# A fused attention and gated feed-forward kernel: one match-row copy moved to ScalarE's queue, one copy moved to VectorE, and the written-out order laid out anew

## The chip, the core and the metric

The kernel runs on one core of one Trainium2 chip. A core has a matrix engine (TensorE, PE in the profile), a vector engine (VectorE, DVE), a scalar engine for activations (ScalarE, ACT), a general engine (GpSimd, POOL) and a synchronization engine (SyncE, SP). SP, ACT and POOL each have a queue from which they start DMA transfers; all transfers are carried by the same 16 DMA engines. Every engine works through its own instructions in their order and waits for the others through semaphores. Times are microseconds of device time of one execution; lower is better.

## What the kernel computes

Attention with routing comes first. Queries and keys are each assigned to the nearest of 16 centroids of their head, and a query sees only the keys of its own centroid. The result feeds a feed-forward layer with a sigmoid gate. Shapes: q, k, v are 4 x 8 x 768 x 64 (batch, head, position, dimension); the tokens are 3072 x 512, the weights 512 x 1536, 512 x 1536 and 1536 x 512.

```python
q_assign = argmax(einsum('bhsd,hcd->bhsc', q_n, c_n), -1)      # q_n, k_n, c_n: normalized
k_assign = argmax(einsum('bhsd,hcd->bhsc', k_n, c_n), -1)
mask = q_assign[:, :, :, None] == k_assign[:, :, None, :]
scores = where(mask, q @ k.T / sqrt(D), -1e9)
attn = softmax(scores) @ v
x = attn.transpose(0, 2, 1, 3).reshape(3072, 512)
out = (sigmoid(x @ w_gate) * (x @ w_val)) @ w_out
```

## The kernel before

**Tiles.** Two heads make a pair, and a batch has four pairs. A pair's queries and keys stand transposed in two tiles, `even` and `odd` (the positions stand in six chunks of 128, and the tiles hold the even and the odd chunks; the columns are the two heads' halves of 384): rows 0 to 63 hold the values, rows 64 to 79 hold the one-hot match rows of the assignment, scaled so that one product of 80 rows gives a score that already carries the mask. The exponentials (L957, ACT) turn score banks `sc` into `es` tiles, the value products (L985, PE) sum them with the V tiles `vp` into the bank `av`; V carries a column of ones, so the sum of the exponentials comes with it. DVE divides (L1010, L1015) into `xn`, which is turned to `x`, mostly by a transposing DMA on SP's queue (L1043), for a few blocks by PE (L1023). The feed-forward part takes x in groups of 256, 512 and then 384 tokens: gate and value projections (L1081) into three banks `ring`, tanh on ACT (L1097), the product on DVE (L1108) into `hT`, the out projection (L1136), a copy on ACT (L1153), a store on SP.

**Match rows.** For the first pair, `prepare_first` (L819) turns keys and queries on PE (L837), copies the four halves out of the banks (L846, a table in line 842 says on which engine: all on ACT), multiplies with the block of centroids (L884), and DVE turns these scores, takes maxima, compares and writes the match rows (`place`, L688, by L515). `place` writes the odd queries' rows first into spare rows of `even` and then copies them to `odd` by a 24 KB DMA (L706, on SP). The other three pairs of batch 0 go through `prepare_pair` (L713: L729, L736 or L518, L769). The later batches go through `prepare` (L520): for two pairs together, matches by L625, and match rows brought by eight DMAs, `even` or `odd` from `oht`; the first two pairs of batch 1 are turned on PE (L555), the others are loaded as quarters (96 KB DMAs in runs of 32 numbers) and turned on DVE (L536). There the rows of `odd` are brought from `even` by a DMA of 192 KB (L592). The DMAs started through the helper `dma` carry its line, 292, in the profile.

**Centroids.** c1 to c5 (L360 to L377) normalize the centroids; c5 turns them on PE (L373), and DVE places them (L382).

**The order.** The kernel does not write its instructions in the order of its loops. Each piece of work is a task with an engine, a length, what it needs, what buffers it takes and a due time (class `Order`, L38). `schedule` (L109) simulates the engines: on each engine, of the tasks that could start first (within 0.02 us), the one with the earliest due time goes next; the queue on SP lets only two of the quarter loads (pkt 13) be under way. `transfers` (L74) shares the DMA time among the queues, with fixed costs in `DMA_START` and `DMA_LAND`. After nine rounds the emitted order is fixed for every engine. Due times come from `due_at` (L277: a line of the place in the attention, with another slope before slot 96) and `due_ffn` (L280), with offsets where work is added.

**What the change touches.** `Order.schedule`, `due_at`, `due_ffn`, the issue lengths (`ISSUE`, L288, and `dma`, L290), `load_nat` (L396), `prepare`'s quarter copies (L541), the match-row due time (L681), `place` (L706), `prepare_first`'s table (L842), `attend` and its end (L919 to L1065), `feed` (L1068), the weight due times `WT` (L1177), `prepare_pair`'s due times (L1188) and the loads of the next batch (L1195 to L1216).

## Time and profile before

| what | value |
|---|---|
| median of 3 runs (lowest, highest) | 325.28 us (324.61, 325.47) |
| the profiled execution's own time | 325.91 us |
| its span | 324.1 us |
| PE busy | 315.6 us, 97% |
| ACT busy | 224.6 us, 69% |
| DVE busy | 147.0 us, 45% |
| POOL busy | 76.2 us, 24% |
| DMA moved | 36.94 MB, mean 114 GB/s |
| mean granted TensorE clock | 0.995 |

The profile is one execution. Its span runs from the first to the last instruction that is recorded; the execution's own time is 1.8 us longer. The busy shares are means over stages that differ: the first 40 us hold the loads and the setup of batch 0, the middle interleaves attention with the feed-forward part, and from about 270 us on the feed-forward part runs alone. In a row of the timeline, the first number is the start, the second how long the merged instructions took, and the bracket tells how long the engine had stood before and what ended that. Rows with SPq or POOLq are DMA issues on these queues.

### The profile page before, as it was taken

The page shows a single profiled execution, that of the slowest core. Times are in us where ns is not written, and L with a number is a line of the kernel's source. Part 1 is how long each engine was busy: PE and PEld are TensorE (multiplying, and loading weights), DVE is VectorE, ACT ScalarE, POOL GpSimd, SP SyncE. Part 2 cuts the span into 40 slices and gives each one's busy share as a digit, 9 for nine tenths or more (in the row PEclk, how much of TensorE's full clock was granted, in tenths as well). Part 3 has the DMA queues.
Part 4 walks back from the last instruction along what each step waited for, and adds up shares of the span by engine and source line. Part 5 has one row for each costly group of instructions (what it writes and reads, how often), then busy time and mean ns, then how long its engine had stood idle before and what let it go on. Part 6 is the DMA issues. An engine that isn't in the chain of part 4 may idle for free.

```text
span 324.1 us, 7275 instructions
## 1 busy us (share of the span) xinstructions
PE 315.6 (97%) x2869; PEld 193.0 (60%) x2869; DVE 147.0 (45%) x344; ACT 224.6 (69%) x326; POOL 76.2 (24%) x121
## 2 busy tenths in 40 slices
PE   8879999999999999999999999999999999999996
PEld 3547888645545656566565655666556665654653
DVE  3859743564954068732433965233113331430430
ACT  5669999438749879797787775888878873332422
POOL 4879661862133115000304061000000000000000
PEclk9979999999999999999999999999999999999999
DMA  6999999947567884226687845200120001002002
GB/s 219 350 248 232 231 218 209 150 98 164 94 145 143 154 156 133 56 48 107 141 185 146 153 104 115 69 15 14 47 77 14 13 14 65 34 0 95 5 0 97
DMA packets 80273, 36.94 MB, mean 114 GB/s; under 512 B 65072, under 2 KB 75056, under 8 KB 80240
## 3 DMA queue, kind: packets, MB, share of 16 engines
q1 hardware_dynamic: 72944, 25.05, 33.1%
q0 software_dynamic: 6864, 11.01, 17.2%
q8 instruction: 22, 0.36, 0.5%
q10 hardware_dynamic: 432, 0.43, 0.4%
q14 instruction: 11, 0.09, 0.1%
HBM read 28.34 MB, written 6.29 MB: 107 GB/s over the span
## 4 chain that ended last, share of the span: by engine, by line
PE 90%; ACT 4%; DMA 3%; DVE 1%; issue 1%; SPq 0%; ACTq 0%
PE ring L1081 38%; PE ring L1136 19%; PE sc L938 18%; PE av L985 10%; ACT es L957 4%; PE sc L625 3%; DMA odd<-even 2%; DMA nat<-in_k_dram 1%; DVE even L515 0%; PE ring L769 0%; PE ring L555 0%; PE ring L884 0%; PE ring L837 0%; DVE ohf L504 0%; PE ring L729 0%
## 5 line engine op out<-in xcount | busy, mean ns | idle before, releaser
L957 ACT ACTIVATE es<-sc,nbias 128x768 f16<-128x768 f32 (+1 forms) x188 | 166.5, 918 | 34.8 <-PE sc L938 33.1
L1108 DVE SCALAR_TENSOR_TENSOR hT<-gt,ring 128x384 f16<-128x384 f32 (+2 forms) x96 | 53.1, 553 | 99.9 <-PE ring L1081 97.4
L1081 PE MATMUL ring<-x,wv 128*128 128x384 f16 (+2 forms) x384 | 78.1, 326 | 0.0
L1081 PE MATMUL ring<-x,wg 128*128 128x384 f16 (+2 forms) x384 | 78.1, 325 | 0.0
L1097 ACT ACTIVATE gt<-ring 128x384 f32<-128x384 f32 (+2 forms) x96 | 47.1, 490 | 32.6 <-DVE hT L1108 16.8
L1136 PE MATMUL ring<-wo,hT 128*128 128x512 f16 (+2 forms) x300 | 69.5, 370 | 0.0
L985 PEld LDWEIGHTS <-es 128*128 128x128 f16 x1152 | 54.9, 97 | 20.7 <-ACT es L957 0.5
L985 PE MATMUL av<-vp,es 128*128 128x65 f16 x1152 | 59.9, 193 | 0.2 <-ACT es L957 0.2
L1081 PEld LDWEIGHTS <-wg 128*128 128x128 f16 x384 | 35.8, 97 | 22.8
L1081 PEld LDWEIGHTS <-wv 128*128 128x128 f16 x384 | 34.8, 97 | 22.0 <-issue 1.2
L1136 PEld LDWEIGHTS <-hT 128*128 128x128 f16 x300 | 27.9, 97 | 27.2
L588 POOL CAST even<-t 128x768 f16<-128x768 f32 x24 | 19.9, 831 | 87.1 <-DVE t L536 69.5
L1153 ACT ACTIVATE osb<-ring 128x512 f32<-128x512 f32 (+2 forms) x25 | 14.5, 580 | 24.7 <-PE ring L1136 24.6
L938 PEld LDWEIGHTS <-even 80*128 80x128 f16 x216 | 19.5, 98 | 15.2 <-issue 6.2
L938 PE MATMUL sc<-odd,even 80*128 80x384 f16 x96 | 26.5, 332 | 1.7 <-DMA odd<-even 1.7
L938 PE MATMUL sc<-even 80*128 80x384 f16 (+2 forms) x120 | 26.5, 294 | 1.1 <-POOL even L757 0.6
L938 PE MATMUL sc<-even,odd 80*128 80x384 f16 (+2 forms) x120 | 26.2, 293 | 0.0
L938 PE MATMUL sc<-odd 80*128 80x384 f16 x96 | 25.9, 327 | 0.2 <-ACT es L957 0.2
L938 PEld LDWEIGHTS <-odd 80*128 80x128 f16 x216 | 19.5, 98 | 9.8 <-issue 1.8
L1010 DVE RECIPROCAL rr<-av 128x6 f32<-128x6 f32 (+2 forms) x36 | 6.8, 190 | 36.9 <-PE av L985 36.7
L536 DVE STREAM_TRANSPOSE t<-nat 128x384 f32<-128x384 f32 x40 | 20.6, 550 | 5.0 <-DMA nat<-in_k_dram 4.8
L462 POOL CAST vp<-nat 128x384 f16<-128x384 f32 x32 | 15.9, 538 | 15.2 <-PE av L985 7.8
(75 smaller groups left out, 168.6 us busy)
## 6 DMA issues: line engine op xcount, KB each, us to landing
out_dram<-osb SPq DMA_DIRECT2D x23, 256.0 KB, 2.1
nat<-in_v_dram POOLq DMA_DIRECT2D x12, 384.0 KB, 4.7
nat<-in_k_dram SPq DMA_DIRECT2D x32, 96.0 KB, 3.0
nat<-in_q_dram SPq DMA_DIRECT2D x32, 96.0 KB, 3.5
odd<-even SPq DMA_DIRECT2D x12, 192.0 KB, 3.8
nat<-in_k_dram SPq DMA_DIRECT2D x5, 384.0 KB, 6.3
nat<-in_q_dram SPq DMA_DIRECT2D x5, 384.0 KB, 7.7
nat<-in_v_dram SPq DMA_DIRECT2D x4, 384.0 KB, 7.6
```

Of the source, the lines that this page charges most:

```text
L462: lambda e=e: nc.gpsimd.tensor_copy(vps[i % NVP][:, e, :, 0:D], buf.tile[:, e, :, :]),
L536: nc.vector.transpose(t[:, half * QB : (half + 1) * QB].rearrange("p (c x) -> p c x", x=128), blocks_[:, half],)
L588: nc.gpsimd.tensor_copy(t[:, NM[nm], cols], t32[p, nm].tile[:, cols])
L625: nc.tensor.matmul(out=ps[32 * g : 32 * g + 32, half, :QB], lhsT=cblk[:, 2 * p + half, :], rhs=t32[p, nm].tile[:, half * QB : (half + 1) * ...
L938: nc.tensor.matmul(out=ps[:, i // per, i % per * N : (i % per + 1) * N], lhsT=kb.tile[0:80, 0, e * QB + j // 2 * 128 : e * QB + (j // 2 + ...
L957: i = nc.scalar.activation(take(es)[:, : together * N].rearrange("p (u c) -> p u c", u=2), sc.tile[:, :, : per * N], AF.Exp, bias=nbias, s ...
L985: nc.tensor.matmul(out=av.tile[:, g : g + D + 1], lhsT=es.tile[:, i * N + c * 128 : i * N + (c + 1) * 128], rhs=vp[:, e, j, :], start=firs ...
L1081: nc.tensor.matmul(out=ps[:, :N], lhsT=ws[fc // FPG][:, dcc, fc % FPG, :], rhs=xb.tile[:, dcc, :N], start=(dcc == 0), stop=(dcc == NDC - 1),)
L1097: lambda rg=rg, gt=gt: nc.scalar.activation(take(gt)[:, :N], rg.tile[:, :N], AF.Tanh, scale=0.5),
L1108: nc.vector.scalar_tensor_tensor(t[:, fc, :N], gt.tile[:, :N], 1.0, rv.tile[:, :N], ALU.add, ALU.mult)
L1136: nc.tensor.matmul(out=ps[:, : m1 - m0], lhsT=hb.tile[:, fc, tb * 128 : (tb + 1) * 128], rhs=wos[fc // FPG][:, fc % FPG, m0:m1], start=(fc ...
L1153: lambda rg=rg, osb=osb, w=m1 - m0: nc.scalar.mul(take(osb)[:, :w], rg.tile[:, :w], 0.5),
```

## The change

It has three parts. The copy of the odd queries' match rows of the first pair is issued on ACT's queue instead of SP's; for the other pairs it stays on SP. The copy of the first pair's second query half out of its bank is made by DVE instead of ACT. The rest changes what the planner assumes and when work is due, and so the order on every engine: engines are free from 0.7 us on, the queue of POOL lets eight transfers be under way, issue lengths and some transfer lengths are other numbers, a set of quarter copies on DVE may not start before the last set has, and due times move. No instruction is added or taken away; the numbers of instructions stay the same on each engine but for the one copy and the one issue.

```diff
+    ROOM = {"SP": 2, "POOL": 8}
...
-        free = {e: 0.0 for e in {t.eng for t in self.tasks}}
-        order, ends = [], []
+        free = {e: 0.7 for e in {t.eng for t in self.tasks}}
+        order, under_way = [], {"SP": [], "POOL": []}
...
-            if t.pkt == 13 and t.eng == "SP":
+            if t.dma and (t.eng == "POOL" or t.eng == "SP" and t.pkt == 13):
+                ends = under_way[t.eng]
                 ends.append(
-                    start + self.DMA_START["SP"] + t.dma if t.landing is None
+                    start + self.DMA_START[t.eng] + t.dma if t.landing is None
                     else start + t.landing - self.DMA_LAND
                 )
-                if len(ends) > 1:
-                    free["SP"] = max(free["SP"], sorted(ends)[-2])
+                room = self.ROOM[t.eng]
+                if len(ends) >= room:
+                    free[t.eng] = max(free[t.eng], sorted(ends)[-room])
...
-    S1, T1 = 96, 51.1
+    S1, T1 = 96, 51.6
-        return T1 + (slot - S1) * (0.442 if slot < S1 else 0.78)
+        return T1 + (slot - S1) * (0.42 if slot < S1 else 0.823)
-        return 36 + work * 1.8
+        return 36 + work * 1.6
-    ISSUE = {"SP": 0.62, "ACT": 0.68, "POOL": 0.85}
+    ISSUE = {"SP": 0.62, "ACT": 0.45, "POOL": 0.76}
...
-                        seq=[cp[p, nm, 0]] if half else [], acq=[] if half else [t32[p, nm]],
+                        seq=[cp[p, nm, 0]] if half else in_turn[-1:],
+                        acq=[] if half else [t32[p, nm]],
                         uses=[natb[b, p, nm]] + ([t32[p, nm]] if half else []),
                     )
+                    if half:
+                        in_turn.append(cp[p, nm, 0])
...
         m = dma(
-            "SP", lambda: od_.tile[64:80, NM["q"], :], lambda: ev.tile[80:96, NM["q"], :], 0.1,
+            "SP" if p else "ACT", lambda: od_.tile[64:80, NM["q"], :],
+            lambda: ev.tile[80:96, NM["q"], :], 0.1,
...
-            on = {("k", 0): "ACT", ("k", 1): "ACT", ("q", 0): "ACT", ("q", 1): "ACT"}[nm, h]
+            on = {("k", 0): "ACT", ("k", 1): "ACT", ("q", 0): "ACT", ("q", 1): "DVE"}[nm, h]
...
-        early = slot < 72.0
+        early = slot < 66.0
-                    due - (28.0 if early else 0.0), lat=0.25,
+                    due - (28.5 if early else 0.0), lat=0.25,
-            due + (-3.1 if last else 4.0) - (18.0 if early else 0.0), lat=0.25 if last else 0.0,
+            due + (-2.6 if last else 4.0) - (23.5 if early else 0.0), lat=0.25 if last else 0.0,
...
-                    "DVE", 0.1 + 0.4 * w, gated, [g2, v1], due - 15.5, lat=0.2, seq=done[:1],
+                    "DVE", 0.1 + 0.4 * w, gated, [g2, v1], due - 11.5, lat=0.2, seq=done[:1],
...
-    WT = (14, 16, 22, 24, 27, 31.5, 38.0, 36, 39)
+    WT = (14, 20.0, 23.5, 24.0, 25.5, 31.0, 38.0, 34.0, 35.0)
...
-        prepare_pair(0, p_, 6.0 * p_, 0.32, (('k', 'q'), (), ('k', 'q'))[p_ - 1], p_ in (1, 2, 3))
+        prepare_pair(0, p_, (0, 6.5, 7.5, 14.0)[p_], 0.31, (('k', 'q'), (), ('k', 'q'))[p_ - 1], p_ in (1, 2, 3))
...
-                            b + 1, p_, nm, "POOL" if (b, grp[0]) == (0, 2) else "SP", max(due - 36.0, 20),
-                            due - 60 if b else 42 if grp[0] else 17.5,
+                            b + 1, p_, nm, "POOL" if (b, grp[0]) == (0, 2) else "SP", max(due - 32.0, 20),
+                            due - 60 if b else 40.0 if grp[0] else 21.5,
-                prepare(b + 1, grp, max(due - 32, 44) + (10 if (b, grp[0]) == (0, 2) else 0), 1.0)
+                prepare(b + 1, grp, max(due - 23.0, 43.5) + (8.0 if (b, grp[0]) == (0, 2) else 0), 1.15)
...
-                    load_v(b + 1, p_, "POOL", due - 26.5, due - 15, due - 39.5)
+                    load_v(b + 1, p_, "POOL", due - 26.5, due - 15, due - 36.0)
```

The due times of the normalization and the turn of x go from 16.0 to 17.5 before the block's, those of batch 0's V casts 6 us later, the match rows' offset from 20 to 22, a POOL quarter's issue from 1.1 to 0.74 and its transfer from 0.55 to 0.7, and a first load's transfer from 0.8 to 0.65.

More of the change, by code (lines that the diff above doesn't have):

```diff
@@ L287 @@
     Q = {"SP": nc.sync, "ACT": nc.scalar, "POOL": nc.gpsimd}
-    ISSUE = {"SP": 0.62, "ACT": 0.68, "POOL": 0.85}
+    ISSUE = {"SP": 0.62, "ACT": 0.45, "POOL": 0.76}
     def dma(eng, out_of, in_of, size, deps=(), due=0.0, acq=(), uses=(), early=0.0, seq=(), pkt=65, lat=0.0):
         return od.add(
-            eng, (1.1 if eng == "POOL" else 0.69) if pkt == 13 else ISSUE[eng], lambda: Q[eng].dma_start(out=out_of(), in_=in_of()),
+            eng, (0.74 if eng == "POOL" else 0.69) if pkt == 13 else ISSUE[eng], lambda: Q[eng].dma_start(out=out_of(), in_=in_of()),
             deps, due, acq=acq, uses=uses, dma=size, early=early, lat=lat, seq=seq, pkt=pkt,
@@ L407, in load_nat @@
                         lambda e=e: src[b, 2 * p + e].rearrange("(p c) d -> p c d", c=NCH),
-                        0.8, (), due[e], acq=[] if e else [buf], uses=[buf] if e else [],
+                        0.65, (), due[e], acq=[] if e else [buf], uses=[buf] if e else [],
                         seq=nat[b, p, nm][:],
@@ L428, in load_nat @@
                         lambda a=a: parts[a // 2, a % 2],
-                        0.55, (), due, acq=[] if a else [buf], uses=[buf] if a else [],
+                        0.7 if eng == "POOL" else 0.55, (), due, acq=[] if a else [buf], uses=[buf] if a else [],
                         early=early, seq=nat[b, p, nm][:1], pkt=13, lat=2.0,
@@ L679, in prepare @@
                                 0.04 if split else 0.07,
-                                [a5, shifted[b, p, half]], due - (20 if (b, grp[0]) == (1, 0) else 0),
+                                [a5, shifted[b, p, half]], due - (22.0 if (b, grp[0]) == (1, 0) else 0),
                                 uses=[oht, aug[b, p][e]], lat=1.5,
@@ L1046, in turn_by_dma @@
             )
-        t4 = od.add("DVE", 0.17 + 0.02 * nq, rec, [t3], due - 16.0, lat=0.05, acq=[rr], uses=[av])
-        t5 = od.add("DVE", 0.14 + 0.15 * nq, norm, [t4], due - 16.0, lat=0.2, acq=[xn], uses=[av, rr])
+        t4 = od.add("DVE", 0.17 + 0.02 * nq, rec, [t3], due - 17.5, lat=0.05, acq=[rr], uses=[av])
+        t5 = od.add("DVE", 0.14 + 0.15 * nq, norm, [t4], due - 17.5, lat=0.2, acq=[xn], uses=[av, rr])
         if not ((b, gr) == (0, 0) and p >= 2 or block == blocks[-1]):
@@ L1058, in attend @@
             return together
-        t6 = od.add("PE", 0.02 + 0.06 * nq, turn, [t5, c_ident16], due - 16.0, lat=0.25, acq=[rg], uses=[xn])
+        t6 = od.add("PE", 0.02 + 0.06 * nq, turn, [t5, c_ident16], due - 17.5, lat=0.25, acq=[rg], uses=[xn])
         xd.append(
             od.add(
-                "DVE", 0.1 + 0.133 * nq, out_of_bank, [t6], due - 16.0, lat=0.2, seq=xd[:1],
+                "DVE", 0.1 + 0.133 * nq, out_of_bank, [t6], due - 17.5, lat=0.2, seq=xd[:1],
                 acq=[] if xd else [xb], uses=[rg] + ([xb] if xd else []),
@@ L1174 @@
         load_nat(0, p_, "q", "SP", -7.9 + p_, behind=nat[0, p_, "k"])
-        load_v(0, p_ - 1, "SP", -7.8 + p_, 9.0 + 4.5 * p_, behind=nat[0, p_, "q"])
-    load_v(0, NP - 1, "SP", -7.7 + p_, 9.0 + 4.5 * NP, behind=nat[0, NP - 2, "v"])
-    WT = (14, 16, 22, 24, 27, 31.5, 38.0, 36, 39)
+        load_v(0, p_ - 1, "SP", -7.8 + p_, 15.0 + 4.5 * p_, behind=nat[0, p_, "q"])
+    load_v(0, NP - 1, "SP", -7.7 + p_, 15.0 + 4.5 * NP, behind=nat[0, NP - 2, "v"])
+    WT = (14, 20.0, 23.5, 24.0, 25.5, 31.0, 38.0, 34.0, 35.0)
     n = 0
```

4 lines of the change are left out of this document (2 added, 2 removed).

## The prediction

> **What bounds the kernel now.** I read the slices of the page first, for where TensorE (PE) and its clock are not full; then the busy times by stage; then the timeline of 4 to 27 us for the one hole they show; then the DMA issues around it, for why.
>
> ```profile
> PE   8879999999999999999999999999999999999996
> ACT  5669999438749879797787775888878873332422
> PEclk9979999999999999999999999999999999999999
> ```
>
> PE is full from the fourth slice to the last; the first three slices, and there the third one's clock, are what is left to win.
>
> ```profile
> 16.00:17.00 1.00, 0.35 (x3) 0.18 (x3) 0.96 (x3) 0.49 (x1) 1.00 (x2) 1.00 1.06 366
> 17.00:18.00 1.00, 0.00 (x0) 0.00 (x0) 0.92 (x3) 0.00 (x0) 1.00 (x3) 0.96 1.15 319
> 18.00:19.00 1.00, 0.98 (x4) 0.47 (x4) 0.19 (x1) 0.15 (x1) 0.94 (x2) 0.50 1.21 208
> 24.00:32.00 8.00, 7.23 (x100) 5.78 (x99) 7.34 (x21) 8.00 (x11) 7.40 (x11) 1.00 0.92 239
> ...
> 80.00:120.00 40.00, 40.00 (x361) 21.79 (x350) 19.32 (x42) 29.00 (x39) 8.88 (x14) 1.00 0.72 137
> ```
>
> Columns: stage, length, busy time of PE, its weight loads, DVE, ACT, POOL, then the clock and the DMA engines. From 16.4 to 18.0 PE and ACT both stand, and at 18 the clock halves; 18 to 21 stays at 0.50, 21 to 22 averages 0.84. From 24 on ACT is full (8.00 of 8), from 42 PE is (40.00 of 40), and it stays so until 321.1, with 3.0 us for the last copy and store. So nothing after 42 us gains unless the work before it gets there sooner, and anything new that stops PE after 42 costs its full length.
>
> ```profile
> 12.07 1.11 ACT L957 ACTIVATE es<-sc,nbias 128x1024 f16<-128x1024 f32 x1 [1.52 <-PE sc L938]
> 13.40 2.12 ACT L957 ACTIVATE es<-sc,nbias 128x1024 f16<-128x1024 f32 x2 [0.21 <-PE sc L938]
> ...
> 18.02 1.12 PE L938 MATMUL sc<-odd,even 80*128 80x384 f16 x3 [1.66 <-DMA odd<-even]
> ...
> 18.85 1.69 ACT L957 ACTIVATE es<-sc,nbias 128x768 f16<-128x768 f32 x2 [1.92 <-PE sc L938]
> ```
>
> The hole is one wait: the scores of the first pair's odd queries wait for their match rows (odd<-even), a DMA.
>
> ```profile
> nat<-in_v_dram SPq DMA_DIRECT2D x1, 384.0 KB, 8.2
> odd<-even SPq DMA_DIRECT2D x1, 24.0 KB, 6.2
> ```
>
> Issued on SP at 11.79, 24 KB land 6.2 us later, at 17.97; the 384 KB load issued before them on the same queue (9.6) lands at 17.8. The rows stood behind loads, not behind their own size.
>
> **The change, part by part.** My sum is made on the profiled execution, 325.91 us (span 324.1, and 1.8 around it); it stands 0.63 above the median, 325.28.
>
> 1. *The start of the first pair.* In the new instruction order the turn of the centroids (L373, waits for DVE until 5.28) goes ahead of the second key turn, which ran at 4.77. The turn is then at 5.34, and the keys and both queries at 5.48, 5.89 and 6.30 (three transposes 0.41). With 0.59 from turn to copy (4.77 to 5.36) ACT's last two copies end at 6.56 and 7.00, and the second query half, now on DVE (0.53 to 0.56 there, 0.49 on ACT), runs 6.89 to 7.44 instead of ending at 6.91. So +0.53 for the match chain on DVE: its first rows are ready at 11.1, not 10.56, the last even query half at 12.3. PE in turn waited until 11.41 for a load, so its next matches (L769) come only 0.1 later and the first exponential starts at 12.26 (+0.19). ACT's table load moves from 6.92 to 7.00.
>
> 2. *The rows' issue on ACT.* In ACT's order it stands behind the first exponential, which ends at 13.37; the rows it reads are ready by 12.3, so it does not wait. Price: ACT's issues in the trace took 0.41 (centroids) and 0.93 for two; bounds 0.41 and SP's 0.61, I take 0.45. Behind it on ACT stand the second and third exponentials, which end at 16.0 instead of 15.52, and for the third the value products wait; these end at 16.25. On SP, the issue goes (0.6), and so does the first early key load of the next batch, which ran at 12.49: its four loads now stand together behind the first transposing DMA, at about 19.3 to 20.8.
>
> 3. *The landing.* A 24 KB row copy behind loads on ACT's queue is not in the trace. Nearest rows: 1.9 us on an emptier queue (66 to 71 us), 3.3 and 4.1 at 25 to 27 us, 6.2 here; ACT's own first load took 2.8. I take 3.0, since ACT's queue holds nothing else: 13.4 + 3.0 = 16.4. Between 1.9 and 6.2 it lands at 15.3 to 19.6; below 16.25 nothing more is won, since PE is busy until then. [...]
>
> 4. *PE and its clock.* The odd scores start at 16.45 instead of 18.02. 3.4 us at half clock cost 1.7 us of PE time; with 0.2 us of idle left instead of 1.66 I expect full clock. [...]
>
> 5. *To the steady stage.* The fourth exponential comes at 17.0 instead of 18.85. Six exponentials (0.85) and four copies (0.49) follow until pair 1's first long one: 17.0 + 7.06 = 24.1, and 0.35 for the third pair's match scores (0.85, L769), which now stand before its scores: 24.45 instead of 25.94, 1.5 us gained. From there ACT ran 14.21 us without a gap; its work is the same, so PE's full stage begins 1.5 us sooner.
>
> 6. *The new order after that.* Same 2,869 products, so its price is only new waits. I measured in PE work, at the chain's paces (65-column product 0.73/24 us, 384-column 0.65/4), how far each consumer stands behind its producer. Score to value products: nowhere under 1.3 us after 36 us of work (1.22 before). Match scores (L625) to the first scores that use them: 10.9, 14.5, 14.5, 14.3, 13.9, 14.3 us (before 12.7, 13.6, 19.3, 18.7, 23.5, 22.4). The needed chain is DVE's eight steps (4.1 to 7), row issues (0.62 each, up to six) and 1.9 to 3 us to land: 10 to 13 us against the odd scores 1 to 1.5 us behind the first. It fits each time, by 1 to 2.5 us. On POOL's queue the second weight (wv) now follows a V load and four casts, so it is issued at about 20.3 instead of 16.3 and lands by 29.8 (9.5 us as before), long before its use at 39.2 (40.7 - 1.5). The first part of wo comes last of the three; the transfer that held that place on POOL's queue before landed at 58.8 (issued 42.2, 16.6 to land), and its use is at 61.2 (62.7 - 1.5). All of this I put at 0, bounds -0.5 and +1.5: cover is the room named, and where it is gone PE stops for what is missing.
>
> The end is unchanged. Sum: 325.91 - 1.5 = 324.4 profiled, and on the median 325.28 - 1.5 = 323.8. In PE work alone the place at 24.3 us would be 2.2 us better, as the third pair's match scores are done by then; ACT's stage gives 0.7 of that back.
>
> **The rivals.**
> - *The first projections wait for the transposed x (slower).* x0's second part goes by transposing DMA on SP; before, it is issued at 31.3 and lands at 38.4, 0.65 ahead of the first projection at 39.05. Now four loads (1.5 MB) stand on SP's queue from 19.3. If they drain by 27.7 (the same bytes as before, with the DMA engines' hole at 28 to 29 filled, 43 and 19 GB/s), x0 lands near 37.0, in time for 37.6 (39.05 - 1.5). If they drain at 31, two transposing DMAs of 4.9 and 4.5 us put it at 40.4: PE stops 2.8 us, net +1.3, 326.6. It decides from a landing of about 39.1 on, where the gain is gone. For it: x DMAs that took 6 to 7 us and halve the rate (205 GB/s at 18 to 23, 390 after). Against: the producer is issued 2 us sooner.
> - *The rows land no sooner on ACT's queue.* 6.2 us from 13.4 is 19.6, fourth exponential at 20.2, 1.3 later than before, clock still dropped: 326.6. For it: DMA engines full (1.06). Against: they landed 0.17 us behind the load before them on SP, as things in one line do. [...]
> - *Hidden or given back.* ACT's full stage or x0 as the gate lets only 0.5 us through: 324.8. For it: PE loses only 1.4 us between 25 and 42, so two engines must both move up.
> - *A new stop in the full stage*, such as the stores (which wait for ACT's copy of the out projection) now ahead of the match rows on SP, once or twice 1 us: 324.8 to 325.8.
>
> **How the numbers follow.** My forecast, a gain of 1.0 to 2.5 us: 0.60. x0 late 0.12 (0.07 of it slower by over 0.3%), rows no sooner 0.08, hidden 0.10, a new stop 0.10 (0.05 of it slower). 0.3%, 0.98 us, is about what a measurement here can tell from no change (the runs span 0.86). Faster: 0.60; slower: 0.07 + 0.08 + 0.05 = 0.20; same the rest, 0.20. Range: low 322.7 (2.2 by PE work and 0.4 in the full stage), high 326.3, which leaves out the upper part of the two slow cases. The likeliest's own range is 322.8 to 324.3.
>
> **What would show it.** Right: odd<-even on ACT's queue landing near 16.4, PE's wait before the odd scores under 0.5, clock 1.00 from 16 to 22, pair 1's long exponentials from 24.5, PE full from about 41. Step 1 shows in the DVE transposes of the first match rows at 11.1. Wrong: a PE wait for x or for odd rows, idle PE anywhere past 42, a landing over 5 us on ACT's queue, or the half clock moved to another window.

## The result, and the profile after

The changed kernel takes 325.64 us in the median of 21 runs (325.03 to 327.49), the kernel before 324.61 beside it (323.32 to 325.84): a ratio of 1.0044, 95% interval 1.0027 to 1.0061. It is slower by 0.44%; the forecast was a gain of 1.5, from 325.28 to 323.8. The profiled execution of it took 325.50 us (span 323.7), so it looks 0.4 better than the 325.91 of the profile before.

Executions of one kernel differ in the mean of TensorE's granted clock (0.999 or 1.00 in 16 of the changed kernel's 21, 0.995 in three, 0.990 in two; the profile before, at 0.995, shows one half step, at 0.50 from 17.9 to 21.3 us), so a median "at full clock" below is that of the executions without such a half step, at 0.998 or more: 324.34 for the kernel before (22 of 30, taken beside the first experiments), 325.53 for the changed one (16 of 21).

The slices of PE, ACT and the clock after:

```profile
PE   7888999999999999999999999999999999999996
ACT  4689999439549996766777777676777677863422
PEclk9999999999999999999999999999999999999999
```

The dip of the clock in the third slice is gone and the third slice of PE is fuller, but the first and the fourth are lower; PE is full from the fifth on, before it was from the fourth. Busy time by stage after, with the columns of the table before:

```profile
16.00:17.00 1.00, 1.00 (x17) 0.86 (x14) 0.99 (x3) 1.00 (x2) 1.00 (x2) 1.00 0.94 140
17.00:18.00 1.00, 0.73 (x11) 0.55 (x12) 1.00 (x3) 0.21 (x1) 1.00 (x3) 1.00 0.79 91
18.00:19.00 1.00, 1.00 (x14) 0.55 (x11) 0.94 (x4) 0.95 (x2) 1.00 (x2) 1.00 1.21 202
24.00:32.00 8.00, 6.54 (x88) 4.87 (x86) 7.16 (x20) 7.26 (x8) 7.56 (x12) 1.00 1.16 271
...
80.00:120.00 40.00, 40.00 (x366) 22.38 (x364) 16.43 (x35) 30.67 (x42) 8.74 (x14) 1.00 0.75 154
```

The hole at 16.4 to 18.0 is gone. A new one is at 24 to 32: PE had 7.23 of 8 us there and has 6.54, ACT had 8.00 and has 7.26. Now the timeline after (its lines of code stand some 7 further down: L945 is L938 before; in the experiments they shift by a few more):

```profile
5.32 0.48 PE L376 MATMUL av<-ident,cn 128*128 128x128 f32 x1 [0.74 <-DVE cn L359]
...
5.59 2.13 PE L844 MATMUL ring<-ident,nat 128*128 128x128 f32 x9
...
13.77 1.11 ACT L964 ACTIVATE es<-sc,nbias 128x1024 f16<-128x1024 f32 x1 [1.92 <-PE sc L945]
...
13.89 0.60 ACTq L295 DMA_DIRECT2D odd<-even  x1
...
15.09 2.12 ACT L964 ACTIVATE es<-sc,nbias 128x1024 f16<-128x1024 f32 x2 [0.21 <-PE sc L945]
...
17.52 0.65 PE L945 MATMUL sc<-odd,even 80*128 80x384 f16 x3
...
18.05 1.69 ACT L964 ACTIVATE es<-sc,nbias 128x768 f16<-128x768 f32 x2 [0.84 <-PE sc L945]
```

The first exponential comes at 13.77, 1.70 later than before, and the odd scores at 17.52, only 0.50 sooner. The rows' issue and landing:

```profile
odd<-even ACTq DMA_DIRECT2D x1, 24.0 KB, 3.5
```

13.89 + 3.5 = 17.4, where 16.4 was forecast.

### The profile page after: what moved, and what is told of

Read it like the earlier page. It is cut to its first block, busy times and chain, and to the rows that moved or that the text cites. A ratio compares the mean times of both kernels' runs of the same rounds, so it can differ in the third digit from the quotient of the medians.

```text
span 323.7 us, 7289 instructions
## 1 busy us (share of the span) xinstructions
PE 315.2 (97%) x2869; PEld 193.2 (60%) x2869; DVE 149.3 (46%) x345; ACT 224.8 (69%) x325; POOL 76.5 (24%) x121
## 3 DMA queue, kind: packets, MB, share of 16 engines
q0 software_dynamic: 6864, 11.01, 17.2%
## 4 chain that ended last, share of the span: by engine, by line
PE 93%; ACT 3%; DVE 1%; DMA 1%; issue 1%; ACTq 0%; DVEq 0%
PE ring L1088 38%; PE ring L1143 19%; PE sc L945 19%; PE av L992 11%; PE sc L631 3%; ACT es L964 3%; DMA cn<-in_centroids_dram 1%; PE ring L776 1%; PE ring L561 1%; PE ring L891 1%; PE ring L844 1%; PE ring L736 0%; DVE ohf L507 0%; DVE even L518 0%; DVE t L493 0%
## 5 line engine op out<-in xcount | busy, mean ns | idle before, releaser
L1143 PE MATMUL ring<-wo,hT 128*128 128x512 f16 (+2 forms) x300 | 71.2, 370 | 0.0
L1088 PEld LDWEIGHTS <-wg 128*128 128x128 f16 x384 | 34.9, 97 | 22.1 <-issue 0.6
L1143 PEld LDWEIGHTS <-hT 128*128 128x128 f16 x300 | 26.6, 97 | 25.7 <-issue 1.2
L945 PE MATMUL sc<-even 80*128 80x384 f16 (+2 forms) x120 | 26.5, 294 | 3.0 <-ACT es L964 1.9
L945 PEld LDWEIGHTS <-even 80*128 80x128 f16 x216 | 19.4, 98 | 15.6 <-issue 2.5
L1160 ACT ACTIVATE osb<-ring 128x512 f32<-128x512 f32 (+2 forms) x25 | 14.5, 580 | 19.5 <-PE ring L1143 17.8
L945 PEld LDWEIGHTS <-odd 80*128 80x128 f16 x216 | 19.7, 98 | 13.6 <-issue 1.4
L945 PE MATMUL sc<-even,odd 80*128 80x384 f16 (+2 forms) x120 | 26.3, 293 | 0.0
L945 PE MATMUL sc<-odd,even 80*128 80x384 f16 x96 | 26.0, 326 | 0.2 <-ACT es L964 0.2
L945 PE MATMUL sc<-odd 80*128 80x384 f16 x96 | 26.0, 325 | 0.0
L465 POOL CAST vp<-nat 128x384 f16<-128x384 f32 x32 | 16.8, 578 | 26.1 <-DMA nat<-in_v_dram 25.9
```

What stands on the lines that cost most here:

```text
L465: lambda e=e: nc.gpsimd.tensor_copy(vps[i % NVP][:, e, :, 0:D], buf.tile[:, e, :, :]),
L945: nc.tensor.matmul(out=ps[:, i // per, i % per * N : (i % per + 1) * N], lhsT=kb.tile[0:80, 0, e * QB + j // 2 * 128 : e * QB + (j // 2 + ...
L1088: nc.tensor.matmul(out=ps[:, :N], lhsT=ws[fc // FPG][:, dcc, fc % FPG, :], rhs=xb.tile[:, dcc, :N], start=(dcc == 0), stop=(dcc == NDC - 1),)
L1143: nc.tensor.matmul(out=ps[:, : m1 - m0], lhsT=hb.tile[:, fc, tb * 128 : (tb + 1) * 128], rhs=wos[fc // FPG][:, fc % FPG, m0:m1], start=(fc ...
L1160: lambda rg=rg, osb=osb, w=m1 - m0: nc.scalar.mul(take(osb)[:, :w], rg.tile[:, :w], 0.5),
```

## The experiments

Most edits move single tasks in the order that is written out and leave everything else where the planner put it:

```diff
         order = self.schedule()
+        for t, o in self.moves:
+            self.put(order, t, o)
         for t in order:
             t.emit()
```

`put` sets task t right behind o, and what needs t behind t. `turns`, `scored_last` and `exps` list the turns of keys and queries, the scores and the value products in the order in which they were made; `quad[p]` is the match products of pair p, `nat` and `vload` are the loads and the casts of V, `x_first` is the first transposing DMA. All times are medians of device time; the ratios are against the kernel before on the same chip. Beside the different experiments the kernel before took 323.9 to 324.3 at full clock, and from 5 in 29 to 11 in 16 of its executions had a half step, so a ratio somewhat under 1 can come from the half steps alone: the medians at full clock decide.

**The start, and the two moves.** First the centroid turn put back behind the second key turn, then the same in reverse in the kernel before, and the two named moves: the rows alone in the kernel before, and both undone in the changed one.

```diff
+    od.moves = [(c5, turns[1])]
```

> The changed kernel with one instruction of TensorE moved: the centroid turn (L376) stands behind the first pair's second key turn (L844), as it did before the change; everything else keeps its place. Theory A (the centroid turn ahead of the second key turn is what costs: TensorE idles 0.74 us for the centroids at 4.58, its clock stays at half pace until 9.24 instead of 4.26, and the first pair's chain runs 1.7 us later): the four match products take about 1.35 us instead of 2.00, the first match rows start near 10.0 instead of 11.9, the first exponential near 12.2 instead of 13.8, pair 1's long exponentials near 23.6 instead of 25.2, and the time is 323.9 to 324.6, 1.0 to 1.7 under the changed kernel's 325.64 and about even with the kernel before or up to 0.7 under it. Theory B (the start is made up for later, and the new order behind 25 us is what costs): 325.3 to 325.8, within 0.3 of the changed kernel.

Measured: 326.43 (ratio 1.0056, 1.0027 to 1.0085), 325.61 at full clock (only 2 of its 7 executions). The first exponential came at 11.58, but the odd scores waited until 16.98 for the rows, and nothing was gained. Theory A falls as an account of the loss.

```diff
+    od.moves = [(turns[1], c5)]
```

> The kernel before with only the centroid turn (L373) moved ahead of the first pair's second key turn. Theory A: TensorE waits for the centroids from about 4.6 to 5.3 and runs at half pace until about 9, the first match rows start near 11.8 instead of 9.8, and, since the moved rows of this kernel stand on SyncE's queue behind the same transfers whatever the start, part of it is hidden behind the row transfer, which would now be issued at about 13.7; the time is 0.8 to 2.0 over the kernel before, 325.4 to 326.6. Theory B: within 0.3 of the kernel before, 324.3 to 324.9.

Measured: 324.26 (0.9995, 0.9975 to 1.0016), 324.14 at full clock: no loss. Here PE waited 0.57 us for the centroids, but ran the nine transposes behind them in 1.15 us, not 2.13, and the first exponential came at 11.72:

```profile
5.07 0.33 PE L376 MATMUL av<-ident,cn 128*128 128x128 f32 x1 [0.57 <-DVE cn L359]
5.23 1.15 PE L840 MATMUL ring<-ident,nat 128*128 128x128 f32 x9
```

So the turn's place alone doesn't make the start late. What differs is when TensorE came to full pace: the trace's record of the full granted clock begins at 4.26 us in the profile before, where the six transposes behind the turn took 0.82 us, and at 9.24 in the profile after, where the nine took 2.13. Over all profiled executions the first exponential lies between 11.58 and 13.77. Whether the turn's place makes a late record likelier is not settled: with the early turn the nine transposes took 1.15 us in this execution, 2.13 in the profile after and 2.04 in the run below that undoes both moves.

```diff
+        if not p:
+            m.emit = lambda: nc.scalar.dma_start(out=od_.tile[64:80, NM["q"], :], in_=ev.tile[80:96, NM["q"], :])
```

(This changes the emission alone, not what the planner assumes; the planned order stays.)

> The kernel before with only the first pair's odd query match rows issued on ScalarE's queue, behind the first exponential; the order on every other engine stays. Theory A: the rows land near 16.0 (issue at about 12.3, then 3.5 us as in the changed kernel), the odd scores start near 16 instead of 18.0, the half-pace stretch at 18 is gone, and the time is 0.5 to 1.7 under the kernel before, 322.9 to 324.1. Theory B, under which this early gain is handed back in the stage behind 25 us: within 0.3 of the kernel before, 324.3 to 324.9.

Measured: 324.32 (0.9997, 0.9978 to 1.0017), 324.24 at full clock. The reason is in its timeline and in the queues' rows for two stretches, 12.3 to 16.2 and 16.2 to 17.3 us (q1 carries what SP issues, q0 POOL, q10 ACT: in the profile before q10 moved 0.43 MB, for 416 KB of loads issued on ACT, and q0 11.01 MB, for 10,752 KB issued on POOL; the columns are packets, MB, share of 16 engines):

```profile
12.32 0.59 ACTq L711 DMA_DIRECT2D odd<-even  x1
...
17.90 0.65 PE L940 MATMUL sc<-odd,even 80*128 80x384 f16 x3 [1.36 <-DMA odd<-even]
```

```profile
q1 hardware_dynamic: 1042, 1.51, 106.4%
```

```profile
q1 hardware_dynamic: 213, 0.31, 92.8%
q0 software_dynamic: 13, 0.01, 8.0%
q10 hardware_dynamic: 32, 0.02, 7.6%
```

For 3.9 us after the issue not one packet of the rows moved; 1,042 of SP's did. The rows landed 5.5 us after their issue, at 17.8, as on SP's queue (17.97).

```diff
+        if not p:
+            m.emit = lambda: nc.sync.dma_start(out=od_.tile[64:80, NM["q"], :], in_=ev.tile[80:96, NM["q"], :])
...
-                f = dve_scaled if on == "DVE" else act_scaled
+                f = act_scaled if (nm, h) == ("q", 1) else act_scaled
```

(Again in the emission alone; all four copies go to ACT.)

> The changed kernel with its two moves undone and its new order kept: the odd query match rows are issued on SyncE's queue again (they stand there ahead of the first transposing transfer) and the second query half is copied by ScalarE. Theory A: the rows are issued only once the transfers ahead of them leave SyncE's queue, and land at 17.5 or later, so nothing is gained by the early issue and the late start is kept: 325.6 to 327.0, that is as slow as the changed kernel or up to 1.4 slower. Theory C (the copy by VectorE, not the order, delays the first pair, as it stands between the centroid work and the match work there): the copy on ScalarE gives back 0.2 to 0.6, 324.8 to 325.4 if the rows land no later.

Measured: 325.81 (1.0050, 1.0024 to 1.0076), 325.64 at full clock, as the changed kernel: the two moves together are worth nothing here, and the new order is what costs, 1.3 us against the kernel before's 324.34 beside it.

**What the landing depends on.** In the changed kernel SP issues two loads of 192 KB and ten of 384 KB before 11.4 us. Two of the ten, the values of pairs 2 and 3, were put behind the first transposing DMA (`x_first`).

```diff
+    od.moves = [(t, x_first) for t in (*nat[0, 3, "v"], *nat[0, 2, "v"])]
```

> The changed kernel with the loads of pair 2's and pair 3's values (the last two of the eleven transfers of 384 KB that SyncE issues before 11.4) put behind the first transposing transfer on SyncE's queue. Theory D (the odd query match rows land only when the loads issued before them have drained, near 16.3, on whichever queue they are): the loads drain near 14.2, the odd scores start at 16.0 to 16.6 instead of 17.5, the fourth exponential at 17.2, right behind the third, instead of 18.05, and the time is up to 0.85 under the changed kernel, 324.7 to 325.3, as long as the values of pairs 2 and 3 still come in time. Rival G (the 3.5 us from issue to landing is ScalarE's queue's own): the odd scores start at 17.5 and the time is 325.5 to 326.5.

Measured: 325.08 (1.0018, 0.9997 to 1.0039), all at full clock, in two groups: five executions took 323.7 to 324.0, seven 325.0 to 325.7, and the profiled one (325.55) is of the second. Its rows' issue, landing, and the scores:

```profile
13.89 0.59 ACTq L305 DMA_DIRECT2D odd<-even  x1
...
17.53 0.65 PE L955 MATMUL sc<-odd,even 80*128 80x384 f16 x3
```

```profile
odd<-even ACTq DMA_DIRECT2D x1, 24.0 KB, 2.0
```

Landed at 15.9 instead of 17.4, as Theory D says, and yet the scores started at 17.53: they stand in PE's order behind the value products of the third exponential, which ended at 17.22 in this execution. There are two gates, and one was still shut. In this execution TensorE was late at full pace (twelve transposes from 9.85 us on took 2.00 us, 0.17 each; in the profile before nine from 8.71 on took 1.20, 0.13 each); the five quicker executions may be those where it came to it sooner, but they were not profiled. Both opened:

```diff
+    od.moves = [(c5, turns[1]), *((t, x_first) for t in (*nat[0, 3, "v"], *nat[0, 2, "v"]))]
```

> The changed kernel with two edits together: the centroid turn behind the second key turn, and the loads of pair 2's and pair 3's values behind the first transposing transfer. Theory I (the odd scores stand behind two gates, the end of the third exponential and its value products, 17.2 in the changed kernel, and the landing of the match rows, 17.4; opening one alone leaves the other): the third exponential ends near 15.0, the rows are issued at 11.7 and land near 15.0, the odd scores start at 15.1 to 15.6 instead of 17.5, the fourth exponential at 15.6 to 16.2 instead of 18.05; if nothing behind takes it back the time is 1.2 to 2.0 under the changed kernel, 323.6 to 324.4. Theory H (the stage from 18 to 26 is bound by something that does not move with these, the copies, casts and loads of the later pairs): the odd scores move, pair 1's first long exponential stays near 25 and the time stays at 325.2 to 325.9.

Measured: 323.93 (0.9969, 0.9945 to 0.9992), 323.78 at full clock: 1.7 under the changed kernel, where the turn alone gave nothing and the loads alone 0.45 in the median. Against the kernel before beside it, 324.02 at full clock, that is 0.2.

```profile
12.78 0.60 ACTq L305 DMA_DIRECT2D odd<-even  x1
...
16.41 0.65 PE L955 MATMUL sc<-odd,even 80*128 80x384 f16 x3
```

With the rows back on SP, and, in another run, with the copy back on ACT (both in the emission alone):

```diff
+        if not p:
+            m.emit = lambda: nc.sync.dma_start(out=od_.tile[64:80, NM["q"], :], in_=ev.tile[80:96, NM["q"], :])
```

```diff
-                f = dve_scaled if on == "DVE" else act_scaled
+                f = act_scaled if (nm, h) == ("q", 1) else act_scaled
```

> The run at 323.93 (centroid turn late, two value loads late) with the odd query match rows back on SyncE's queue, ahead of the first transposing transfer. If the issuing queue is without weight once nothing stands ahead of the rows (Theory I): the odd scores start within 0.3 us of 16.4, right behind the third exponential, and the time is 323.6 to 324.3. If ScalarE's queue itself is the quicker (Theory G): the odd scores start at 17.0 or later and the time is 324.4 to 325.2.

> The run at 323.93 with the second query half copied by ScalarE again, behind the other three copies, as before the change. If the copy is on no path that ends last (what the prediction said of it, at most 0.1 us): 323.6 to 324.3. If VectorE's copy starts the match chain earlier or later than ScalarE's by more than 0.3 us, the first exponential moves by as much and with it the time, 323.4 to 324.7.

Measured: 323.43 (0.9957, 0.9937 to 0.9976) and 323.90 (0.9973, 0.9951 to 0.9995). So it makes no difference which engine makes the copy (323.86 at full clock against 323.78). The first is the best version found, faster than both kernels (323.28 at full clock, against 324.21 of the kernel before beside it); its rows, on SP's queue but with eight loads of 384 KB ahead instead of ten, land sooner (15.3) than any on ACT's queue behind ten or more (16.9 to 17.8):

```profile
11.81 0.60 SPq L728 DMA_DIRECT2D odd<-even  x1
...
15.45 0.65 PE L957 MATMUL sc<-odd,even 80*128 80x384 f16 x3
```

```profile
odd<-even SPq DMA_DIRECT2D x1, 24.0 KB, 3.5
```

The gates side by side, from the profiled executions; the last column is the span less the start of the fourth exponential:

| kernel | rows issued | landed | third exponential ends | odd scores | fourth exponential | from it to the end |
|---|---|---|---|---|---|---|
| before | 11.79, SP | 17.97 | 15.52 | 18.02 | 18.85 | 305.3, half clock in it |
| before, rows on ACT | 12.32, ACT | 17.8 | 15.70 | 17.90 | 18.42 | 304.2 |
| the same, one load late | 12.08, ACT | 17.1 | 15.47 | 17.16 | 17.68 | 304.2 |
| after | 13.89, ACT | 17.4 | 17.21 | 17.52 | 18.05 | 305.7 |
| after, turn back | 11.71, ACT | 16.9 | 15.03 | 16.98 | 17.50 | 306.9, half clock in it |
| after, two loads late | 13.89, ACT | 15.9 | 17.22 | 17.53 | 18.06 | 305.7 |
| both | 12.78, ACT | 15.1 | 16.10 | 16.41 | 16.94 | 305.9 |
| both, rows on SP | 11.81, SP | 15.3 | 15.14 | 15.45 | 15.97 | 305.4 |

In the new order the odd scores start 0.31 after the third exponential's end or within 0.1 of the landing, whichever is later; in the three rows of the old order the landing is the later one. The last column is the second finding: at full clock the profiled executions of the new order take 305.4 to 306.1 from the fourth exponential on, the two of the old order's 304.2.

**What the order loses.** 1.27 us lies between the fourth and the tenth exponential: 7.12 us in the new order, 5.85 in the old (kernel before, rows on ACT). The new order:

```profile
23.46 0.97 ACT L964 ACTIVATE es<-sc,nbias 128x768 f16<-128x768 f32 x1
...
24.00 0.85 PE L776 MATMUL ring<-t,cblk 128*32 128x384 f32 x8
...
25.17 4.13 ACT L964 ACTIVATE es<-sc,nbias 128x1024 f16<-128x1024 f32 x4 [0.74 <-PE sc L945]
...
26.33 0.27 PE L945 MATMUL sc<-even 80*128 80x256 f16 x1 [0.64 <-ACT es L964]
...
27.43 0.49 PE L945 MATMUL sc<-even 80*128 80x256 f16 x3 [0.50 <-ACT es L964]
```

The old order in the same stage:

```profile
24.27 5.19 ACT L959 ACTIVATE es<-sc,nbias 128x1024 f16<-128x1024 f32 x5
...
24.80 0.85 PE L771 MATMUL ring<-t,cblk 128*32 128x384 f32 x8
...
26.04 0.82 PE L555 MATMUL ring<-ident,nat 128*128 128x128 f32 x6
```

In the new order pair 3's match products stand inside pair 1's first bank of scores, ACT waits 0.74, and then PE has nothing left between exponentials; in the old order these products and the next batch's first transposes fill the gaps. ACT also makes one copy (0.49) more before the tenth exponential, and no run moved that copy alone. From the fourth to the twenty-second exponential 1.1 of the 1.27 is still there. Pair 3's products were moved back, first in part, then wholly:

```diff
+    od.moves = [(quad[3], exps[8])]
```

> The changed kernel with the four match products of pair 3 (the third group of L776) behind pair 1's first bank of scores, the first two scores of its second bank and the value products behind these, instead of inside the first bank; nothing else moves. Theory D (the early moves are hidden behind the landing of the loads, and the new order loses 1.1 us later: 0.74 where ScalarE has no scores at 24.4 because TensorE does these match products first, 0.4 in two stops at 50 and 55): the first long exponential of pair 1 starts near 24.4 instead of 25.2, ScalarE's 0.74 us pause before it is gone, and the time is 0.5 to 0.9 under the changed kernel's 325.64, 324.7 to 325.1. Rival F (the pause only moves the work that TensorE has to do anyway, and comes back in front of the next exponentials): 325.4 to 325.9.

```diff
+    od.moves = [(quad[3], scored_last[31])]
```

> The changed kernel with pair 3's match products behind the whole first and second bank of pair 1's scores, where the kernel before has them (with them between the two halves of the second bank the pause had only moved from the first long exponential to the second). Theory D: from the ninth exponential (23.46) to the second of the long ones takes 2.0 instead of 2.7, and the time is 0.5 to 0.9 under the changed kernel, 324.7 to 325.1. Theory F (TensorE has this work to do anyway, and the pause turns up at the next bank): 325.4 to 325.9.

Measured: 325.84 (1.0044, 1.0025 to 1.0064) and 325.90 (1.0032, 1.0011 to 1.0054). Nothing. In the second the ninth to the eleventh exponential took 2.10 us instead of 2.72, but the pause was back at the fourteenth (1.49 us after the thirteenth instead of 1.00). Then this move added to the two that opened the gates:

> The changed kernel with the three edits together: the centroid turn and pair 3's match products back in their old places, the values of pairs 2 and 3 behind the first transposing transfer. Theories I and D: the gains add, 323.0 to 323.8, about 2 under the changed kernel and 0.8 to 1.5 under the kernel before. Theories H and F: 325.0 to 325.9. One of the two pairs only: 323.9 to 325.0.

Measured: 324.29 (0.9983, 0.9958 to 1.0008), no better than without. The reverse, in the kernel before:

```diff
+    od.moves = [(quad[3], scored_last[26])]
```

> The kernel before with only the four match products of pair 3 (the third group of L769) moved forward, into pair 1's first bank of scores, where the changed kernel has them. Theory D: pair 1's first long exponential starts 0.6 to 0.9 later than without the move, measured from the fourth exponential, and the time is 0.5 to 0.9 over the kernel before, 325.2 to 325.6. Rival F: within 0.3 of the kernel before, 324.3 to 325.0.

Measured: 326.16 (1.0046, 1.0023 to 1.0068), 325.62 at full clock. In it pair 3's match products stand ahead of a copy that completes their input, so they read an input that is not complete; the instructions and their number are the same. The ninth to the tenth exponential took 2.01 us instead of 1.16, but what ACT waited for there is not what it waits for in the new order: the copy itself stood behind the products.

```profile
24.56 0.49 ACT L746 ACTIVATE t<-ring 128x384 f32<-128x384 f32 x1 [0.69 <-PE ring L779]
```

So this run does not show what the products' place costs by itself, and undoing it in the new order doesn't take the loss back. Then the other difference, the next batch's keys and their transposes, on top of the two moves that opened the gates:

```diff
+    od.moves = [..., *((t, nat[0, 3, "q"][-1]) for t in nat[1, 0, "k"]), (turns[16], scored_last[31]), (turns[17], scored_last[35])]
```

> The changed kernel with the centroid turn and the two value loads late, as in the run at 323.93, and besides the next batch's first key load ahead of the first transposing transfer and its two transposes of keys (L555 of the kernel before, L561 of the changed one) right behind pair 1's second and third bank of scores. Theory J (the new order's loss is work of the next batch that no longer fills TensorE's pauses between exponentials, because its load is issued at 20.6 instead of 10.5): the pauses of 0.80 and 0.66 shrink by 0.6 to 0.7 in all, and the 0.49 us wait for the keys at 28.7 is gone; the time is 0.4 to 1.0 under 323.93, 322.9 to 323.5, if the one load more ahead of the match rows does not bring their landing behind the third exponential. Theory K (the order's loss is elsewhere): 323.7 to 324.4.

Measured: 324.45 (0.9978, 0.9959 to 0.9997), all at full clock, and not under 323.93 (the kernel before beside it took 324.21 at full clock). Theory J falls too: by the starts of PE's instructions the run gained 0.3 us on the one at 323.93 up to 28 and gave 0.2 of it back by 44. Which of the new order's many numbers costs the 1.2 us is not settled.

**Whether the old order gains from the landing.** First the kernel before with the rows on ACT and one, two or three loads behind the first transposing DMA:

```diff
+    od.moves = [(t, x_first) for t in (*nat[0, 3, "v"],)]
```

```diff
+    od.moves = [(t, x_first) for t in (*nat[1, 0, "k"], *nat[0, 3, "v"])]
```

```diff
+    od.moves = [(t, x_first) for t in (*nat[1, 0, "k"], *nat[0, 3, "v"], *nat[0, 2, "v"])]
```

> The kernel before with the odd query match rows on ScalarE's queue and only pair 3's value load behind the first transposing transfer (with the next batch's first key load behind it as well TensorE, in the old order, waited 3.0 us for these keys at 26). Theory I: one load less drains ahead of the rows, 1.0 us sooner; the odd scores start near 16.9 instead of 17.9, the fourth exponential near 17.4 instead of 18.4, and the time is 0.6 to 1.0 under 324.32, 323.3 to 323.8. Theory G: 324.0 to 324.7.

Measured, pair 3's values late: 323.89 (0.9972, 0.9948 to 0.9995). All are at full clock, where the kernel before beside it took 324.21. The fourth exponential came 0.74 sooner than with all loads in place, and the end 0.73 sooner: in these two executions the old order passes it on whole. The medians at full clock differ by 0.36 (324.24 and 323.89).

> The kernel before with the match rows issued on ScalarE's queue and two loads (the next batch's first keys and pair 3's values, not pair 2's, whose cast GpSimd has at 20.6 ahead of pair 3's casts) behind the first transposing transfer. Theory I: the loads ahead of the rows drain near 15.2 instead of 17.2, the rows land near 16.0, the odd scores start at 16.0 to 16.7 instead of 17.9 and the fourth exponential at 16.5 to 17.2 instead of 18.4; the time is 1.0 to 1.8 under the same kernel with all loads in their old place (324.32), 322.5 to 323.4, and faster than both kernels. Theory H: 324.0 to 324.6.

Measured, the next batch's keys late as well: 326.40 (1.0053, 1.0023 to 1.0084). PE stopped for these keys:

```profile
28.93 1.54 PE L565 MATMUL ring<-ident,nat 128*128 128x128 f32 x6 [3.02 <-DMA nat<-in_k_dram]
```

> The kernel before with the first pair's odd query match rows issued on ScalarE's queue, and the last three loads that SyncE issues before 11 (the values of pairs 2 and 3 and the next batch's first keys) put behind the first transposing transfer. Theory D: the rows, issued at 12.3, no longer stand behind these loads (which drained at 17.2), so that the odd scores start at 15.2 to 16.0 instead of 17.9 and the fourth exponential right behind the third, near 15.8 instead of 18.4; the time is 1.5 to 2.6 under the same kernel with the loads in their old place (324.32), 321.8 to 322.8. Rival G: the odd scores stay at 17.5 or later and the time is 324.0 to 324.7.

Measured, pair 2's values late too: 327.57 (1.0106, 1.0075 to 1.0137). The last two runs, with the rows on SP and only the two value loads late, and then with POOL's casts of pair 2's values behind those of pair 3 (`third`) as well, show what holding back pair 2's values costs:

```diff
+    od.moves = [*((t, third[-1]) for t in reversed(vload[0, 2])), *((t, x_first) for t in (*nat[0, 3, "v"], *nat[0, 2, "v"]))]
```

> The kernel before with one edit: the loads of pair 2's and pair 3's values behind the first transposing transfer on SyncE's queue; the odd query match rows stay on SyncE's queue and now stand there behind nine transfers of 384 KB instead of eleven, and ahead of the next batch's first keys. Theory I with a cost of the new order: the rows, issued near 11.8, land before the third exponential's value products are done, the odd scores start at 15.4 to 16.1 instead of 18.0, the fourth exponential at 15.9 to 16.7 instead of 18.4 to 18.9, and all of it stays: 1.7 to 2.4 under the kernel before's runs without the clock's half step (323.4 to 325.2), 321.8 to 323.0. If the sooner start is itself what is paid back between 18 and 65 (by work that finds no pause, or by the values of pair 2 coming late, whose cast stands on GpSimd's queue at 20.6 ahead of pair 3's casts): 323.0 to 324.3.

Measured: 326.17 (1.0045, 1.0019 to 1.0070). All of the 1.7 us was there up to the fifteenth exponential (27.66, instead of 29.34 with the rows on ACT and all loads in place), and then POOL stood for pair 2's values, ahead of pair 3's casts:

```profile
25.73 1.28 POOL L472 CAST vp<-nat 128x384 f16<-128x384 f32 x2 [5.58 <-DMA nat<-in_v_dram]
```

> The run before this one (the kernel before with pair 2's and pair 3's value loads behind the first transposing transfer) with GpSimd's two casts of pair 2's values moved behind the four casts of pair 3. If the old order keeps what it gains: the odd scores start at 15.4 to 16.2, the fourth exponential at 15.9 to 16.8, the sixteenth at 27.9 to 28.8 instead of 31.4, and the time is 322.0 to 323.2, faster than both kernels and than 323.43. If something else stops it behind 25 (the values of pair 2 wanted by TensorE near 28, the next batch's keys at 27): 323.4 to 325.0.

Measured: 325.15 (0.9989, 0.9965 to 1.0013); only 4 of the 12 executions are at full clock. The next stop was PE's, for the next batch's queries:

```profile
28.93 0.87 PE L565 MATMUL ring<-ident,nat 128*128 128x128 f32 x3 [1.80 <-DMA nat<-in_q_dram]
```

So the old order needs its loads where they are: with two or three behind, one is wanted before it has landed. The new order turns the next batch's first keys only from 29 on, and has that room.

## Why the prediction was wrong

- **Step 3, the landing, failed.** It was put at 3.0 us because ACT's queue holds nothing else, the author's estimate from rows that took 1.9 to 4.1 us on SP's queue and a first load of 2.8 on ACT's. Behind all the loads the rows took 3.5 to 5.5 us on ACT's queue: 3.5 in the profile after, where they landed at 17.4, not 16.4. What they waited for is the loads issued ahead of them: on ACT's queue they landed at 17.8 in the kernel before, on SP's at 17.97, and with two loads fewer ahead at 15.9 in the changed kernel. With every load in place the profiles put the landing on ACT's queue at 16.9, 17.4 and 17.8. That was the second rival's mechanism; its price, 6.2 us from the new issue at 13.4, was too high: the issue was at 13.89, and the landing 3.5 us behind it.
- **The new order was the term that turned the sign.** The sum had 0.35 for it in step 5 (the third pair's match scores) and 0 in step 6, bounds -0.5 and +1.5. From the fourth exponential on it costs 1.2 to 1.9 us (305.4 to 306.1 against 304.2), 1.5 in the profile after; between the medians at full clock the order alone costs 1.3 (325.64 against 324.34). 1.27 of it lies between the fourth and the tenth exponential, which is step 5's stage, and by the starts of PE's instructions 0.4 lies in stops between 50 and 56, two of them of 0.21; some came back in between. Step 6's check of distances between producers and consumers looked behind 36 us of PE's work; most of the loss lies ahead of that, where ACT and PE take turns at being the limit. Which part of the order brings it stays open.
- **Steps 4 and 5** had the half clock's 1.7 us as won. That less idle time would keep the clock full was the author's expectation; the profile before has a hole of 1.66 us and the half step, the profile after neither. So it was won there (the fourth to the tenth exponential took 7.12 us where 7.41 was forecast), but the execution it was won against is one of those that have it: 61 of the 162 of the kernel before beside the experiments. Without it the old order takes 5.85 there, not 7.09, so most runs of the kernel before had no such loss to give back. The median that the 1.5 was taken from, 325.28 of three runs, was 324.61 in the 21 beside the changed kernel. That 7.12 came near 7.41 is luck: step 5 added whole lengths (0.85 and 0.49), while from start to start an exponential took 0.79 and a copy 0.37 (at 18.42, 20.00 and 20.37 in the kernel before with the rows on ACT). Six and four of these make 6.2; most of the rest is ACT's wait of 0.74, where the sum had 0.35.
- **Step 1.** The centroid turn ran at 5.32 (5.34 forecast). The first exponential was 1.70 later, not 0.19, because the full clock came only at 9.24 us in this execution; the sum had no term for that, and whether the early turn makes it likelier is open, as said above. By itself the turn's place made no difference to the time either way. It became worth something only when the rows landed sooner (323.93 against 325.08).
- **Step 2** was right that the issue costs nothing on the path; it took 0.60, not 0.45.
- Of the rivals, "rows land no sooner" came true in its mechanism, though not in its price, and "given back" in that the gain was lost between 18 and 42 us; the forecast had priced each by itself and left both small (0.08 and 0.10). No stop for the transposed x showed.

## What to carry to other kernels

A small transfer that landed late behind loads was not helped by another queue here (24 KB at 17.8 us on ACT's, 17.97 on SP's); count the bytes issued ahead of it, and hold back those that nobody wants yet (two loads of 384 KB fewer: 15.9 instead of 17.4), after looking who waits for them next. Where two gates end within 0.2 us of each other (17.21 and 17.4 here), an edit to either may show little or nothing in the median, so open both before giving one up (nothing and 0.45 us for one, 1.7 for both). A gain that is reckoned against one profiled execution must be checked for what that execution alone has, here a half step of the clock.

## What was not expected of the hardware

- In the kernel before with the rows on ACT, 1,042 packets of SP's queue and none of ACT's moved in the 3.9 us after the rows' issue, while loads issued earlier were under way; in the 1.1 us after that, 213 of SP's and all 32 of ACT's. In the changed kernel, with the issue at 13.89, 517 of SP's and none of ACT's moved up to 15.8, and all 32 between 15.8 and 17.0; with two loads fewer ahead none moved up to 15.1, and all 32 between 15.1 and 15.5.
- ACT's DMA issue, behind the first exponential in its order, started 0.12 us after that exponential did (13.89 and 13.77), not at its end.
- A start that is sooner while the rows are not opens a hole before the odd scores, and the half clock came with it: the changed kernel, without a hole in its profile, had a half step in 5 of 21 executions, with the turn alone moved back (hole 1.47 us) in 5 of 7, with the rows' landing moved as well (no hole) in 1 of 12. In the profile before a hole of 1.66 us stands ahead of the half step; with the turn alone moved back the eight match products behind the hole, at 18.05, took 1.43 us, and 0.85 at 18.97 in the kernel before with the rows on ACT, where a hole of 1.36 us was followed by none (mean clock 1.00).
